# State products, folds and token-mixing subtractions on VectorE alone, in a scan, FFT and mixer kernel

## The chip, the cores and the metric

The kernel runs on one core of a Trainium2 chip. Its core has five engines that work beside one another: TensorE (PE, with weight loads on their own row, PEld), VectorE (DVE), ScalarE (ACT), GpSimd (POOL), and SyncE (SP), which issues the DMAs. The metric is the device time of one launch in microseconds (us), lower is better. Three launches of the kernel before took 1111.71, 1112.63 and 1117.65 us; the median is 1112.63 us.

## The reference

```
# q, k, v, a: 4 batches, 8 heads, 768 tokens, 48 channels (d_model = 8*48 = 384)
a_n = a * min(|a|, 0.999) / (|a| + 1e-6)          # complex decay
for t in range(768):
    S = a_n[t] * S + k[t] v[t]^T                  # complex 48x48 state per batch, head
    y[t] = q[t] @ S.real
x = y as (4, 768, 384)
mixed = real(fft over channels(fft over tokens(x)))
u = x + mixed;  un = layernorm(u)
x = u + relu(un @ w_ch1) @ w_ch2                  # 384 -> 1536 -> 384
u = x + (relu(x^T @ w_tok1) @ w_tok2)^T           # 768 -> 256 -> 768 over tokens
out = u + relu(u @ w_ch1') @ w_ch2'               # 384 -> 1536 -> 384
```

## The kernel before, in words

The four batches go one after the other through a chain, and the chain of batch b+1 runs beside the dense layers of batch b.

The chain has two stages. `stage1` first walks 49 scan steps (decay products on VectorE, L407 to L426, fed by ScalarE and GpSimd) and transposes the scaled queries and keys on TensorE (L445). Then come eight chunks of 96 tokens. For each chunk TensorE makes the scores (L511, masked on VectorE in L518), the chunk's own state (`ch_u`, L526 and L527, into PSUM) and the outputs (`ch_y`, L560 and L566, copied into `xT` by ScalarE, L568). The state is carried from chunk to chunk by five instructions in `ch_u`: `Aa` = carried state + new state (L537), three products with the complex decay of a whole chunk (`Xx` in L543, the two halves of `yc` in L544 and L545), and the sum `T` (L547), which the next chunk's L537 and L566 read.

`stage2` does the FFTs as matrix products after folding by symmetry. `xT` is folded into `xm` and `xp` (L784, difference and sum of its token halves), these into `xd` (L790), these into `fd` (L801, eight tiles of four types). TensorE multiplies the folds by cosine and sine tables (L824, L835), ScalarE and GpSimd combine the results (L871 to L873), VectorE adds them to x as `u` (L887), and the normalised rows are transposed (L708, split into a high and a low part in L711 and L712).

The dense layers are `mlp` (L728 and L744, with ScalarE's L732, VectorE's L734 and the residual sum L747), `tok1` (the input is split into `xh` on ScalarE, L933, and `xl` = u - xh, L934; then L949) and `tok2` (L967). Weights come as 64-bit patterns and are turned into two float parts per block by `convert`: ScalarE L187 and L188, VectorE L190, GpSimd L192, VectorE L195, ScalarE L201, GpSimd L202, and a DMA back to DRAM (L203). This happens once, during the chunks and folds of batch 0 and the scan of batch 1.

GpSimd's share in what the change touches: L545 for every chunk but the first, L544 also from batch 1 on; in the folds, the sum `xp` of L784, in L790 the two tiles of `xp` (batch 0) or one of them (later), in L801 two of eight tiles from batch 1 on; and L934 for every batch but 0.

Nobody writes the order of an engine's instructions out. Each instruction gets a priority from its stream (on TensorE the chain goes before dense work; on the others dense work goes first, except in batch 0) and its place in the program, and the framework fixes each engine's order ahead of time from priorities and modelled times. On the chip every engine works through its list in that order.

## Time and profile before

| What | us |
|---|---|
| median of three launches (lowest, highest) | 1112.63 (1111.71, 1117.65) |
| profiled execution, its own time | 1115.16 |
| its span, first to last instruction | 1113.4 |
| TensorE matmuls busy in the span | 991.1 (89%) |
| VectorE busy | 795.6 (71%) |
| ScalarE busy | 517.8 (47%) |
| GpSimd busy | 372.7 (33%) |
| mean granted TensorE clock, 1 = 2.4 GHz | 0.956 |

The profiled execution is 2.5 us over the median. The span starts with batch 0's chain alone (0 to 195.8 us). The first dense matmul is at 195.8; batch 1's folds start at 417.6, batch 2's at 602.2, batch 3's at 806.2; from 852 us to the end TensorE is full with dense layers that depend on no chain any more. A row of the timeline gives start, length, engine, line, operation, written tile, read tiles, shapes and the count of instructions merged into it, and in brackets how long the engine stood idle before and what ended that. A row of grouped lines gives the sum of busy time in us and the mean length in ns.

### The profile page before, as it was taken

The page shows a single profiled execution, that of the slowest core. Times are in us where ns is not written, and L with a number is a line of the kernel's source. Part 1 is how long each engine was busy: PE and PEld are TensorE (multiplying, and loading weights), DVE is VectorE, ACT ScalarE, POOL GpSimd, SP SyncE. Part 2 cuts the span into 40 slices and gives each one's busy share as a digit, 9 for nine tenths or more (in the row PEclk, how much of TensorE's full clock was granted, in tenths as well). Part 3 has the DMA queues.
Part 4 walks back from the last instruction along what each step waited for, and adds up shares of the span by engine and source line. Part 5 has one row for each costly group of instructions (what it writes and reads, how often), then busy time and mean ns, then how long its engine had stood idle before and what let it go on. Part 6 is the DMA issues. An engine that isn't in the chain of part 4 may idle for free.

```text
span 1113.4 us, 21166 instructions
## 1 busy us (share of the span) xinstructions
PE 991.1 (89%) x7322; PEld 924.0 (83%) x7322; DVE 795.6 (71%) x2161; ACT 517.8 (47%) x1442; POOL 372.7 (33%) x510
## 2 busy tenths in 40 slices
PE   1347887999889998799998999999986999999997
PEld 0126775889888897699998899999976999999997
DVE  6996897899999759899876879996565433433332
ACT  7762445777786325777522557651224212121111
POOL 4321896674567336223325312221332002000000
PEclk9997887999999999899999999999988999999999
DMA  6116973587657765264586336655421543544432
GB/s 215 41 38 137 255 265 142 177 273 235 199 190 242 213 170 190 56 202 148 175 199 184 102 99 190 191 171 149 122 79 43 158 127 115 170 142 135 163 100 74
DMA packets 102466, 174.67 MB, mean 157 GB/s; under 512 B 11216, under 2 KB 63568, under 8 KB 101840
## 3 DMA queue, kind: packets, MB, share of 16 engines
q1 hardware_dynamic: 102352, 173.24, 51.4%
q8 instruction: 60, 0.98, 0.4%
q14 instruction: 54, 0.44, 0.1%
HBM read 133.88 MB, written 39.32 MB: 156 GB/s over the span
## 4 chain that ended last, share of the span: by engine, by line
PE 64%; DVE 8%; DMA 3%; ACT 1%; POOL 1%; issue 1%; SPq 0%; POOLq 0%; DVEq 0%; ACTq 0%
PE l L744 23%; PE l L728 22%; PE s L511 3%; PE s L445 2%; DMA cvt<-wL 2%; PE s L835 2%; PE s L560 2%; PE s L824 1%; PE s L566 1%; PE s L949 1%; DVE ws L784 1%; DVE ws L790 1%; PE s L526 1%; PE s L967 1%; PE s L708 1%
## 5 line engine op out<-in xcount | busy, mean ns | idle before, releaser
L744 PE MATMUL l<-w,h 128*128 128x384 f32 x1728 | 331.0, 344 | 12.8 <-DVE h L734 8.8
L728 PE MATMUL l<-th,w 128*128 128x384 f32 x1152 | 313.8, 342 | 5.3 <-DVE h L734 2.6
L744 PEld LDWEIGHTS l<-w,h 128*128 128x128 f32 x1728 | 302.8, 191 | 17.8 <-DVE h L734 12.4
L728 PEld LDWEIGHTS l<-th,w 128*128 128x128 f32 x1152 | 210.3, 189 | 9.4 <-DVE h L734 4.4
L732 ACT ACTIVATE h<-l 128x384 fp32r<-128x384 f32 x192 | 94.1, 490 | 226.0 <-PE l L728 225.2
L728 PE MATMUL l<-tl,w 128*128 128x384 f32 x576 | 194.8, 338 | 0.0
L734 DVE SCALAR_TENSOR_TENSOR h<-l,h 128x384 fp32r<-128x384 f32 x192 | 106.1, 552 | 87.9 <-ACT h L732 87.4
L747 DVE TENSOR_TENSOR u<-u,l 128x384 f32<-128x384 f32 x192 | 105.4, 550 | 76.5 <-PE l L744 75.4
L445 PE MATMUL s<-misc,y 128*112 128x128 f32 x384 | 71.0, 306 | 60.0 <-DVE y L423 38.3
L445 PEld LDWEIGHTS s<-misc,y 128*112 128x112 f32 x384 | 50.2, 148 | 77.1 <-POOL A L384 17.6
L728 PEld LDWEIGHTS l<-tl,w 128*128 128x128 f32 x576 | 108.8, 189 | 0.7 <-DVE tl L712 0.5
L192 POOL TENSOR_TENSOR cvt<-cvt 128x384 int32<-128x384 int32 x56 | 64.4, 1156 | 37.5 <-ACT sq L351 8.1
L366 POOL TENSOR_TENSOR tm<-tm 128x144 f32<-128x144 f32 (+1 forms) x68 | 35.3, 519 | 101.1 <-ACT tm L365 100.9
L511 PE MATMUL s<-qkt 112*96 112x96 f32 x512 | 59.9, 267 | 7.4 <-DVE sc L518 6.7
L511 PEld LDWEIGHTS s<-qkt 112*96 112x96 f32 x512 | 53.6, 177 | 10.6 <-DVE sc L518 7.5
L410 DVE TENSOR_TENSOR p<-p,A 128x144 f32<-128x144 f32 x192 | 59.5, 310 | 3.0
L202 POOL TENSOR_TENSOR w<-cvt,w 128x384 fp32r<-128x384 f32 x44 | 52.6, 1204 | 8.9 <-ACT w L201 8.7
L544 POOL TENSOR_TENSOR yc<-Aa,gm 48x384 f32<-48x384 f32 x18 | 21.0, 1165 | 101.4 <-DVE Aa L537 101.4
L384 POOL TENSOR_TENSOR A<-raw,tm 128x144 f32<-128x144 f32 (+1 forms) x68 | 34.9, 513 | 59.2 <-DVE tm L382 33.2
L195 DVE SCALAR_TENSOR_TENSOR cvt<-cvt 128x384 int32<-128x384 int32 x56 | 46.8, 843 | 8.7 <-POOL cvt L192 8.5
L414 DVE TENSOR_TENSOR p<-p,yt 128x96 f32<-128x96 f32 x192 | 50.1, 261 | 3.5
L934 POOL TENSOR_TENSOR xl<-u,xh 128x384 fp32r<-128x384 f32 x18 | 18.0, 1009 | 101.1 <-ACT xh L933 101.1
(182 smaller groups left out, 1805.1 us busy)
## 6 DMA issues: line engine op xcount, KB each, us to landing
w<-wscr SPq DMA_DIRECT2D x180, 384.0 KB, 3.5
cvt<-wL SPq DMA_DIRECT2D x56, 384.0 KB, 5.1
wscr<-w SPq DMA_DIRECT2D x44, 384.0 KB, 3.7
kn<-y SPq DMA_DIRECT2D x128, 96.0 KB, 2.1
Kn<-kn SPq DMA_DIRECT2D x64, 192.0 KB, 3.9
raw<-aL SPq DMA_DIRECT2D x52, 144.0 KB, 3.1
xx<-xL SPq DMA_DIRECT2D x52, 144.0 KB, 3.1
V<-vL SPq DMA_DIRECT2D x32, 144.0 KB, 3.5
```

What stands on the lines that cost most here:

```text
L192: x = ge.tensor_tensor(out=a, in0=a, in1=lo, op=ALU.add)
L195: rest(ve.scalar_tensor_tensor(out=a, in0=hi, scalar=-0x80000000, in1=a, op0=ALU.bitwise_and, op1=ALU.bitwise_or))
L202: ge.tensor_tensor(out=parts[:, 1, :], in0=a.bitcast(F32), in1=r32(parts[:, 0, :]), op=ALU.subtract)
L410: x = ve.tensor_tensor(out=cur, in0=prev, in1=A[:, j, 0:3, :], op=ALU.mult)
L414: ve.tensor_tensor(out=cur[:, 0:2, :], in0=cur[:, 0:2, :], in1=y, op=ALU.add)
L445: te.transpose(ps[:, j, :], y[:, j, 0:112], ident)
L511: te.matmul(out=ps[:, j, :], lhsT=K[:, hc, :], rhs=Q[:, hc, :])
L728: te.matmul(out=ps, lhsT=w1[:, wi, kt * 128:kt * 128 + 128], rhs=x[g][:, kt, :], start=(n == 0), stop=(n == 8))
L732: x = se.activation(out=hi, in_=ps, func=ACTF.Relu)
L734: ve.scalar_tensor_tensor(out=h[:, 1, g * 384:g * 384 + 384], in0=ps, scalar=0.0, in1=r32(hi), op0=ALU.max, op1=ALU.subtract)
L744: te.matmul(out=ps, lhsT=hs[m][:, hi, tt * 128:tt * 128 + 128], rhs=w2[:, wi, :], start=(n == 0), stop=(n == 8))
L747: ve.tensor_tensor(out=u[tt], in0=u[tt], in1=ps, op=ALU.add)
```

## The change

Every instruction named above as GpSimd's in the chunk products, the folds and `tok1` is issued on VectorE. What is computed, all tiles and all DMAs stay the same. The three tables that held the choice go, and since one of them was a line of its own, every line number behind it is smaller by one in the changed kernel (L545 is L544 there).

```diff
-XL = (0,), (0, 1, 2, 3, 4, 5)
...
-KT, PF, PD = (0, 1), ((2, 0), (2, 1)), (((1, 0), (1, 1)), ((1, 1),))
+KT = (0, 1)
...
-            (ge if c and b else ve).tensor_tensor(out=v8(y)[0:48], in0=a[64:112], in1=gb(1, 64, 112), op=ALU.mult)
-            st["yop"] = (ge if c else ve).tensor_tensor(out=v8(y)[64:112], in0=a[0:48], in1=gb(1, 0, 48), op=ALU.mult)
+            ve.tensor_tensor(out=v8(y)[0:48], in0=a[64:112], in1=gb(1, 64, 112), op=ALU.mult)
+            st["yop"] = ve.tensor_tensor(out=v8(y)[64:112], in0=a[0:48], in1=gb(1, 0, 48), op=ALU.mult)
...
-                x1 = (ge if s else ve).tensor_tensor(out=x[:, :, o:n], in0=xT[:, :, o:n], in1=xT[:, :, 384 + o:384 + n], op=op)
+                x1 = ve.tensor_tensor(out=x[:, :, o:n], in0=xT[:, :, o:n], in1=xT[:, :, 384 + o:384 + n], op=op)
...
-                    x1 = (ge if (s, r) in PD[b > 0] else ve).tensor_tensor(out=xd[s][r][:, :, o:n], in0=x[:, 0:2, o:n], in1=x[:, 2:4, o:n], op=op2)
+                    x1 = ve.tensor_tensor(out=xd[s][r][:, :, o:n], in0=x[:, 0:2, o:n], in1=x[:, 2:4, o:n], op=op2)
...
-                    x = (ge if (ty, r) in PF and b else ve).tensor_tensor(out=fd[:, ty, r, :, lo - sh:hi - sh], in0=xd[s][r][:, :, lo:hi],
+                    x = ve.tensor_tensor(out=fd[:, ty, r, :, lo - sh:hi - sh], in0=xd[s][r][:, :, lo:hi],
...
-            (ve if b in XL[0] and i in XL[1] else ge).tensor_tensor(out=xl[i], in0=u[i], in1=r32(xh[i]), op=ALU.subtract)
+            ve.tensor_tensor(out=xl[i], in0=u[i], in1=r32(xh[i]), op=ALU.subtract)
```

With other engines and other modelled times the orders come out anew. Three places matter below.

First, VectorE in the middle of batch 0's chunks, one chunk long (`cvt` is a weight block in conversion, `sc` the masked scores). Before:

```order
L190 TENSOR_SCALAR cvt<-cvt 128x384 x2
L195 SCALAR_TENSOR_TENSOR cvt<-cvt 128x384
L537 TENSOR_TENSOR Aa<-T,l 112x384
L195 SCALAR_TENSOR_TENSOR cvt<-cvt 128x384
L543 TENSOR_TENSOR Xx<-Aa,gm_81 112x384
L544 TENSOR_TENSOR yc_80<-Aa,gm_81 48x384
L547 TENSOR_TENSOR T<-Xx,yc_80 112x384
L518 TENSOR_TENSOR sc<-s,misc 96x384 x2
```

With the change:

```order
L194 SCALAR_TENSOR_TENSOR cvt<-cvt 128x384
L189 TENSOR_SCALAR cvt<-cvt 128x384 x2
L194 SCALAR_TENSOR_TENSOR cvt<-cvt 128x384
L536 TENSOR_TENSOR Aa<-T,l 112x384
L542 TENSOR_TENSOR Xx<-Aa,gm_81 112x384
L543 TENSOR_TENSOR yc_80<-Aa,gm_81 48x384
L544 TENSOR_TENSOR yc_80<-Aa,gm_81 48x384
L546 TENSOR_TENSOR T<-Xx,yc_80 112x384
L517 TENSOR_TENSOR sc<-s,misc 96x384 x2
```

The second product now stands on VectorE between the first and the sum, which read what GpSimd made before.

Second, VectorE in batch 3's folds (`u_664x` is the dense layer's residual of batch 2). Before:

```order
L734 SCALAR_TENSOR_TENSOR h<-l,h 128x384
L784 TENSOR_TENSOR ws<-xT 112x4x288
L784 TENSOR_TENSOR ws<-xT 112x4x96
L790 TENSOR_TENSOR ws<-ws 112x2x288 x2
L747 TENSOR_TENSOR u_6643<-u_6643,l 128x384
L790 TENSOR_TENSOR ws<-ws 112x2x96 x2
L790 TENSOR_TENSOR ws<-ws 112x2x288
L747 TENSOR_TENSOR u_6644<-u_6644,l 128x384
L790 TENSOR_TENSOR ws<-ws 112x2x96
L801 TENSOR_TENSOR ws<-ws 112x2x191 x4
L747 TENSOR_TENSOR u_6645<-u_6645,l 128x384
L801 TENSOR_TENSOR ws<-ws 112x2x191 x2
```

With the change:

```order
L746 TENSOR_TENSOR u_6646<-u_6646,l 128x384
L783 TENSOR_TENSOR ws<-xT 112x4x288 x2
L783 TENSOR_TENSOR ws<-xT 112x4x96 x2
L746 TENSOR_TENSOR u_6647<-u_6647,l 128x384
L789 TENSOR_TENSOR ws<-ws 112x2x288 x2
L746 TENSOR_TENSOR u_6648<-u_6648,l 128x384
L789 TENSOR_TENSOR ws<-ws 112x2x288 x2
L789 TENSOR_TENSOR ws<-ws 112x2x96 x4
L800 TENSOR_TENSOR ws<-ws 112x2x191 x8
```

All twenty folds are VectorE's now, and of the six residual sums four stand before the folds, where before none did.

Third, TensorE at the same place, from the end of the last chunk to the first products of the folds (`l<-w,h` is a dense layer's second matmul). Before:

```order
L560 MATMUL s<-sc,V 48x96
L566 MATMUL s<-qkt,T 64x96
L566 MATMUL s<-qkt,T 48x96
L744 MATMUL l<-w,h 128x384 x45
L824 MATMUL s<-dcos,ws 128x97 x12
L744 MATMUL l<-w,h 128x384 x9
L824 MATMUL s<-dcos,ws 128x97 x4
```

With the change:

```order
L559 MATMUL s<-sc,V 48x96
L565 MATMUL s<-qkt,T 64x96
L565 MATMUL s<-qkt,T 48x96
L743 MATMUL l<-w,h 128x384 x14
L823 MATMUL s<-dcos,ws 128x97 x16
L823 MATMUL s<-dcos,ws 64x97 x8
L823 MATMUL s<-dcos,ws 65x97 x4
```

Of the 54 dense matmuls that stood behind the last chunk 14 are left there; the other 40 now come earlier. Counted the same way over the whole list, the dense matmuls issued by the end of the last chunk are 876 before and 879 now in batch 1, 1473 and 1506 in batch 2, 2250 and 2290 in batch 3.

## Rows read from the trace of the kernel before

**Rows 1.** Windows: start:end, length, then PE, PEld, DVE, ACT, POOL busy, clock, DMA.

```profile
0.00:195.80 195.80, 118.73 (x963) 91.25 (x963) 161.82 (x452) 109.23 (x315) 103.69 (x143) 0.87 0.53 155
417.60:463.70 46.10, 35.41 (x205) 29.55 (x206) 41.33 (x122) 27.92 (x87) 23.03 (x32) 0.87 0.42 131
463.70:602.20 138.50, 138.45 (x1261) 133.84 (x1260) 111.51 (x346) 73.51 (x214) 39.51 (x67) 0.99 0.60 168
602.20:806.20 204.00, 200.74 (x1626) 191.64 (x1627) 162.18 (x484) 103.14 (x303) 56.89 (x92) 0.98 0.53 153
806.20:852.10 45.90, 34.05 (x196) 28.85 (x197) 30.52 (x65) 16.67 (x45) 19.19 (x18) 0.84 0.15 49
```

**Rows 2.** The same view for batch 0's later chunks and folds.

```profile
107.50:161.90 54.40, 46.10 (x553) 40.39 (x552) 50.64 (x76) 24.36 (x55) 47.41 (x38) 0.82 0.94 286
```

**Rows 3.** Grouped lines of VectorE in that stretch.

```profile
L544 DVE TENSOR_TENSOR yc<-Aa,gm 48x384 f32<-48x384 f32 x6 | 7.4, 1240 | 0.1
L547 DVE TENSOR_TENSOR T<-Xx,yc 112x384 f32<-112x384 f32 x6 | 6.5, 1078 | 1.3 <-POOL yc L545 0.7
...
L801 DVE TENSOR_TENSOR ws<-xd 112x382 f32<-112x382 f32 x8 | 6.2, 842 | 0.0
...
L543 DVE TENSOR_TENSOR Xx<-Aa,gm 112x384 f32<-112x384 f32 x6 | 5.9, 980 | 0.0
L790 DVE TENSOR_TENSOR xd<-xf 112x192 f32<-112x192 f32 x8 | 5.0, 674 | 0.0
```

**Rows 4.** Grouped lines of GpSimd in that stretch.

```profile
L202 POOL TENSOR_TENSOR w<-cvt,w 128x384 fp32r<-128x384 f32 x8 | 13.8, 1735 | 0.0
L192 POOL TENSOR_TENSOR cvt<-cvt 128x384 int32<-128x384 int32 x10 | 12.4, 1252 | 0.4
L790 POOL TENSOR_TENSOR xd<-xf 112x192 f32<-112x192 f32 x8 | 6.8, 876 | 0.1
L545 POOL TENSOR_TENSOR yc<-Aa,gm 48x384 f32<-48x384 f32 x6 | 6.6, 1100 | 33.8 <-DVE Aa L537 31.3 <-ACT w L201 2.3
L784 POOL TENSOR_TENSOR xf<-xT 112x384 f32<-112x384 f32 x4 | 5.8, 1462 | 0.0
```

**Rows 5.** Timeline: VectorE's products and folds where GpSimd was idle.

```profile
105.04 0.55 DVE L545 TENSOR_TENSOR yc<-l,gm 48x384 f32<-48x384 f32 x1
...
427.37 0.75 DVE L790 TENSOR_TENSOR ws<-ws 112x576 f32<-112x576 f32 x1
...
816.76 0.35 DVE L790 TENSOR_TENSOR ws<-ws 112x192 f32<-112x192 f32 x1
```

**Rows 6.** Grouped lines of VectorE in batch 3's folds, 806.2 to 822.2 us.

```profile
L784 DVE TENSOR_TENSOR ws<-xT 112x384 f32<-112x384 f32 x1 | 3.0, 3034 | 0.0
...
L784 DVE TENSOR_TENSOR ws<-xT 112x1152 f32<-112x1152 f32 x1 | 1.4, 1357 | 1.7 <-PE s L566 1.7
```

**Rows 7.** Timeline of TensorE in the folds of batches 1, 2 and 3.

```profile
418.59 3.29 PE L744 MATMUL l<-w,h 128*128 128x384 f32 x18
424.90 4.75 PE L744 MATMUL l<-w,h 128*128 128x384 f32 x18 [3.02 <-DVE h L734]
...
438.12 2.53 PE L824 MATMUL s<-dcos,ws 112*64 112x97 f32 x24 [0.92 <-ACT ws L826]
...
608.01 2.33 PE L744 MATMUL l<-w,h 128*128 128x384 f32 x8 [2.07 <-DVE h L734]
611.54 3.57 PE L744 MATMUL l<-w,h 128*128 128x384 f32 x10 [1.19 <-DVE h L734]
...
814.42 6.10 PE L744 MATMUL l<-w,h 128*128 128x384 f32 x18 [3.42 <-DVE u L747]
...
824.62 4.13 PE L824 MATMUL s<-dcos,ws 112*128 112x97 f32 x40
```

**Rows 8.** Timeline of GpSimd: the first combination in batch 0, and tok1's subtractions.

```profile
179.26 0.53 POOL L872 TENSOR_TENSOR ws<-ws 128x193 f32<-128x193 f32 x1
...
843.24 5.77 POOL L934 TENSOR_TENSOR xl<-u,xh 128x384 fp32r<-128x384 f32 x6 [2.84 <-ACT xh L933]
```

## The prediction

> **What bounds the kernel now.** I read the windows first, cut where the chains meet the dense layers. In the first 195.8 us TensorE is busy for 118.7 and part of that is filler: batch 0's chain runs alone and VectorE, busy for 161.8, sets the pace [rows 1]. Between the folds of batches 1 and 2 and again up to those of batch 3 the picture turns round: TensorE is busy for 138.45 of 138.50 us, then for 200.74 of 204.00, so there only its amount of work counts. The windows of batch 1's and batch 3's folds are the other kind: 35.41 of 46.10 us and 34.05 of 45.90 busy, a clock of 0.87 and 0.84, TensorE waiting for the chain [rows 1]. So the change is paid or earned in four places, batch 0's chunks and folds and three later folds, and TensorE's order decides what is carried between them.
>
> Next the grouped lines of batch 0's stretch. VectorE is busy for 50.64 of 54.40 us and GpSimd for 47.41 [rows 2]: both are full, which looks as if nothing could move. But the lengths say otherwise. A product of 384 columns takes 0.55 us where GpSimd is idle [rows 5]; in this stretch L544 takes 1.24, L547 1.08 and L543 0.98, L801 0.84, and L790's 192 columns 0.67 instead of 0.35 [rows 3, 5]. In batch 3's folds the 384-column L784 takes 3.03 us while the one with 1152 columns before it takes 1.36 [rows 6]. What these share is that both inputs lie in SBUF and that GpSimd runs beside them.
>
> That is a lock and not a slow operation, and the Trainium skill says so (SBUF — State Buffer, "Who interferes with whom"): a VectorE instruction with two SBUF inputs and a GpSimd instruction that reads SBUF hold one port pair in turns, each for its whole length. The trace agrees with the 3.03 against 0.55 us.
>
> **The change, step by step.** It is priced against the profiled execution, 1115.2 us.
>
> *A, batch 0's chunks and folds.* GpSimd loses six L545, four L784 and eight L790: 6.6 + 5.8 + 6.8 = 19.2 us of its 47.4 [rows 2, 4]. VectorE gains ten instructions at 0.55 and eight at 0.35, 8.3 us [rows 5]. How much of VectorE's waiting goes is what the trace does not show, so I bound it. Its waits in these rows are 6 x 0.69 + 6 x 0.53 + 6 x 0.43 + 8 x 0.29 + 8 x 0.32 = 14.8 us, and 54.4 - 50.6 = 3.8 us of idleness come on top: 18.6. GpSimd keeps its twenty conversions there. If waits fall only as its work falls, by 19.2 of 47.4 or 40%, VectorE saves 7.5 and the change costs 0.8. If the two were strictly in turns, all 19.2 go for 8.3: a gain of 10.9. I take a gain of 4.5, near the middle: behind the chunks GpSimd has no conversion left in its list until the folds are through, so the folds run at VectorE's own prices, while in the chunks the conversions still take their turns. The conversions behind the folds, which keep GpSimd until L872 at 179.26 [rows 8], are as many as before and only shift. **-4.5.**
>
> *B, from there to batch 1's folds.* No changed instruction but batch 1's chunk products; three more dense matmuls stand ahead of the folds, at 3.29 / 18 = 0.18 us [rows 7]. **+0.5.**
>
> *C, batch 1's folds.* TensorE's dense work stops for 3.02 us for an L734 that stands behind L784 and L790, and restarts slowly: 18 matmuls in 4.75 us against 3.29 [rows 7]. With the change that L734 comes behind four L784 and one L790 and ends 2 x 1.36 + 2 x 0.55 + 0.75 + 0.55 = 5.1 us after the folds begin, where TensorE now goes on after 424.90 - 417.60 = 7.3, and all folds cost VectorE 3.8 + 4 x 0.75 + 4 x 0.35 + 8 x 0.55 = 12.6 us without a wait [rows 5, 6]. TensorE's last L824 now ends at 440.65, 23.0 us after the start [rows 7]. After the change the 57 dense matmuls left ahead of it (of 936 by then) need 57 x 0.18 = 10.3 us and a wait of about 1, and 64 products at 4.13 / 40 = 0.10 us bring that to some 18: about 4.5 us sooner at best. ScalarE's copies already cost 0.92 us there, so I take 3.5, with 1.5 as the poor end. **-3.5.**
>
> *D, up to batch 2's folds.* TensorE is full, and 1506 instead of 1473 dense matmuls stand ahead of the folds; batch 1 started level, so 33 x 0.18 = **+5.9.** The two products of each chunk and batch 1's six L934 come to VectorE here, but it is busy for only 111.5 of 138.5 us [rows 1], and TensorE's full list hides them; without that cover the 18 chunks of three batches would cost 18 x 2 x 0.55 = 20 us and each batch's L934 3.3.
>
> *E, batch 2's folds and up to batch 3's.* Between the two folds 784 dense matmuls replace 777, +1.3. TensorE stops there now for 2.07 and 1.19 us for L734, and the 18 matmuls behind these take 5.90 us instead of 3.1 [rows 7]: 6.1 us lost. With the change the residual sums stand between the folds instead, and TensorE has three accumulators to run ahead with; I expect about 1.6 us of standstill and 1 of slow restart. So -3.5 + 1.3 = **-2.2**, between -4.8 (nothing lost) and +1.3 (as much as now).
>
> *F, batch 3's folds to the end of its chain.* Only 14 dense matmuls are left here, so TensorE is through them after 2.4 us and idles until the first folds are made, at 3.8 + 4.4 + 2 x 0.55 + 1.1 = 10.4 us. Its restart runs at the lower clock level: after 3.42 us of idleness now, 18 matmuls took 6.10 us, 0.34 each, which is 1.2 instead of 2.4 GHz [rows 7]. The last fold is due at 12.6 + 1.1 = 13.7 us, forty L824 follow at 0.10, plus 1 to 3 us for the slow part: near 19.5 us, where it is 828.75 - 806.2 = 22.5 now. The six L934 among the norm's small steps cost VectorE 6 x 0.55 = 3.3 us in place of a GpSimd run of 5.77 us [rows 8] that held them up; I set that even. **-3.0**, between -6 and +3.
>
> Behind 852 us all is TensorE's and unchanged; SP's list only swaps neighbours. The sum is -4.5 + 0.5 - 3.5 + 5.9 - 2.2 - 3.0 = **-6.8 us**: 1108.4 for the profiled execution, and since the median of 1112.6 lies 2.5 below that one, 1105.8 for the median. A measurement of this kernel tells about 0.5% from no change, 5.6 us, so 1107.0 and 1118.2 are the bounds.
>
> **The rivals.**
>
> *Slower: the filler is spent too early.* TensorE's dense work is what fills the folds. The new order puts 40 of its matmuls ahead of batch 3's folds, where TensorE is full, and takes them from a stretch where it would otherwise stand. Then D's 5.9 and E's 1.3 are paid in full, E's 6.1 comes back at the new standstill, F's idleness of some 8 us makes all 64 L824 run at 0.2 us, 10.4 + 12.8 + 2 of copies = 25.2 against 22.5 and so about +3, and C keeps 1.5: -4.5 + 0.5 - 1.5 + 5.9 + 1.3 + 3 = +4.7, so 1117.3. For it: the counts, the full windows and the slow restarts [rows 1, 7]. Against it: the folds get shorter whatever TensorE does. It decides once TensorE's gap before batch 3's first L824 passes the 3.42 us of now by more than the folds' gain.
>
> *The same: VectorE is saturated in batch 0.* A is +0.8, with the conversions taking every freed turn; with the others as forecast -1.5, so 1111.1. For it: VectorE's 50.64 of 54.40 and GpSimd's 26 us of conversions [rows 2, 4]. The Trainium skill (Perfetto Trace Analysis, "Optimizing Scalar/DVE Operations") speaks for it too: work may be offloaded to GpSimd where VectorE is saturated, though the shared port may spoil that. The 0.55 against 1.24 us says here that it does.
>
> *Much faster: strict turns.* A at -10.9, C at -4.5, E at -4.8, F at -6: with B and D -19.8, so 1092.8. By the rule of the SBUF page, taken to the letter for every instruction, A is this -10.9 and the sum with the rest as forecast -13.2, an estimate. Against it: VectorE's 50.6 us less its 14.8 of waits and GpSimd's 47.4 make 83 in a stretch of 54.4 [rows 2, 3], so much of GpSimd's time was not VectorE's loss.
>
> **How the numbers follow.** Forecast 0.45, slower rival 0.20, same rival 0.20, much faster 0.15. The forecast is good to about 5 us, so 0.28 of it is faster by over 0.5% and 0.17 within; the same rival gives 0.05, 0.13 and 0.02; the slower one 0.02, 0.04 and 0.14; the last is all faster. Faster 0.50, same 0.34, slower 0.16. The range leaves out half of the fast case and a little of the slow one: 1095 to 1119.
>
> **What would show it.** In the new profile L543, L544 and L547 of batch 0's chunks should still show waits, about 0.8 us each, and L790 and L801 0.35 and 0.55; the first dense matmul should come at 191 instead of 195.8. Batch 1's first to last fold should take about 14 us and its last L824 end within 20. Batch 2's folds should begin some 1 to 2 us earlier than 602.2 and show no idle row over 2 us; batch 3's should begin near 802 and show a long gap of TensorE before the first L824. I am wrong if the first dense matmul does not come earlier, if the fold windows are no shorter, or if TensorE shows gaps between 464 us and batch 3's folds that it does not have now.

## The result, and the profile after

The changed kernel is slower: 1125.78 us (median of four launches, 1125.23 to 1129.05) against 1112.17 us (four launches of before), a ratio of 1.0115 with a 95% interval of 1.0090 to 1.0141. The prediction was 1105.8 us, with 1095 to 1119 as its range. The profiled execution of the changed kernel took 1125.23 us, its span is 1123.4 us against 1113.4: 10.0 us more, which is what the views below can account for. The other 3.6 us of the medians' difference lie in the choice of the profiled executions: that of before is 3.0 us above its median, that of the changed kernel 0.6 below.

The first part of the page gives busy time, share and instructions of each engine: GpSimd lost 102 us of work, VectorE gained 24, TensorE is as before.

```profile
PE 988.2 (88%) x7322; PEld 922.6 (82%) x7322; DVE 819.7 (73%) x2251; ACT 514.5 (46%) x1442; POOL 271.0 (24%) x420
```

The windows of the changed kernel, cut at its own landmarks (columns as in [rows 1]):

```profile
0.00:202.80 202.80, 115.64 (x963) 89.99 (x963) 165.19 (x471) 110.01 (x315) 83.63 (x125) 0.88 0.51 150
107.50:161.90 54.40, 42.40 (x548) 38.24 (x547) 52.91 (x95) 24.98 (x55) 26.68 (x20) 0.86 0.94 284
174.90:187.70 12.80, 12.23 (x34) 7.74 (x33) 4.26 (x9) 2.33 (x6) 7.65 (x9) 0.50 0.73 274
425.10:467.50 42.40, 33.49 (x200) 27.22 (x200) 37.80 (x124) 26.20 (x83) 13.09 (x23) 0.88 0.44 143
467.50:617.20 149.70, 147.05 (x1295) 142.42 (x1296) 124.69 (x373) 74.93 (x221) 22.75 (x51) 0.98 0.57 161
617.20:818.80 201.60, 199.70 (x1633) 190.41 (x1633) 165.86 (x502) 101.29 (x300) 37.31 (x74) 1.00 0.52 151
818.80:863.40 44.60, 30.10 (x157) 24.52 (x157) 25.96 (x74) 16.67 (x45) 3.05 (x6) 0.74 0.14 51
```

Held against [rows 1], the prediction's six stretches and the rest behind batch 3's chain come out so:

| Stretch | before | changed | difference | forecast |
|---|---|---|---|---|
| A: to the first dense matmul | 195.8 | 202.8 | +7.0 | -4.5 |
| B: to batch 1's folds | 221.8 | 222.3 | +0.5 | +0.5 |
| C: to the next dense matmul | 46.1 | 42.4 | -3.7 | -3.5 |
| D: to batch 2's folds | 138.5 | 149.7 | +11.2 | +5.9 |
| E: to batch 3's folds | 204.0 | 201.6 | -2.4 | -2.2 |
| F: to the end of batch 3's chain | 45.9 | 44.6 | -1.3 | -3.0 |
| the rest | 261.3 | 260.0 | -1.3 | 0 |

B, C and E are as forecast. In TensorE's timeline C's pauses are 1.64 and 0.37 us where one of 3.02 stood [rows 7], and F has the long pause before the first fold product that was expected:

```profile
430.47 3.39 PE L743 MATMUL l<-w,h 128*128 128x384 f32 x18 [1.64 <-DVE h L733]
434.23 3.42 PE L743 MATMUL l<-w,h 128*128 128x384 f32 x18 [0.37 <-DVE u L746]
437.49 7.12 PE L823 MATMUL s<-dcos,ws 112*128 112x97 f32 x64
...
828.77 12.21 PE L823 MATMUL s<-dcos,ws 112*128 112x97 f32 x64 [7.44 <-ACT ws L807]
```

The loss is in A and D.

**A, up to the last fold.** The window from 107.5 to 161.9 us ends with the last fold in both kernels: nothing was won. The last sum of the chunks (L546) ends at 150.1 us instead of 149.0 (L547), and what the chunks lost the folds won back. Single executions differ here: in seven profiles whose order is that of before up to the last fold it ends at 160.2 to 161.9 us (mean 161.1), in five with the changed order at 159.2 to 162.1 (mean 160.9). GpSimd's work in the window fell from 47.4 to 26.7 us, VectorE's rose from 50.6 to 52.9 [rows 2]. VectorE's grouped lines there say why, and behind them stands all that GpSimd still does:

```profile
L543 DVE TENSOR_TENSOR yc<-Aa,gm 48x384 f32<-48x384 f32 x6 | 7.6, 1271 | 0.1
L544 DVE TENSOR_TENSOR yc<-Aa,gm 48x384 f32<-48x384 f32 x6 | 6.9, 1155 | 0.1
L546 DVE TENSOR_TENSOR T<-Xx,yc 112x384 f32<-112x384 f32 x6 | 6.1, 1015 | 0.2
...
L542 DVE TENSOR_TENSOR Xx<-Aa,gm 112x384 f32<-112x384 f32 x6 | 5.0, 838 | 0.1
L789 DVE TENSOR_TENSOR xd<-xf 112x192 f32<-112x192 f32 x16 | 4.6, 349 | 0.0
...
L800 DVE TENSOR_TENSOR ws<-xd 112x382 f32<-112x382 f32 x8 | 3.8, 555 | 0.0
```

```profile
L191 POOL TENSOR_TENSOR cvt<-cvt 128x384 int32<-128x384 int32 x10 | 12.8, 1294 | 29.4 <-DMA Kn<-kn 29.4
L201 POOL TENSOR_TENSOR w<-cvt,w 128x384 fp32r<-128x384 f32 x8 | 10.3, 1286 | 11.3 <-ACT w L200 8.5 <-DMA Kn<-kn 2.7
L201 POOL TENSOR_TENSOR cvt<-cvt 128x384 fp32r<-128x384 f32 x2 | 3.9, 1964 | 3.0 <-ACT cvt L200 3.0
```

The folds came down to VectorE's own prices, 0.35 and 0.55 us [rows 3, 5]. The products of the chunks did not: L543, the L544 of before, takes 1.27 us where it took 1.24, and the moved product L544 takes 1.16. GpSimd's conversions, twenty instructions as before, took the turns that its products had left.

**A, behind the last fold.** From there to the first dense matmul it took 34.0 us before and takes 41.0. This difference is steady: in the four other runs below whose batch 0 is that of before it takes 33.6 to 33.8 us, in two with the changed batch 0 40.9 and 42.1. TensorE's timeline (start, length):

```profile
169.52 0.83 PE L823 MATMUL s<-dcos,ws 112*65 112x97 f32 x8
173.90 1.09 PE L823 MATMUL s<-dcos,ws 112*63 112x97 f32 x8 [3.54 <-ACT ws L825]
174.92 3.83 PE L834 MATMUL s<-ws 128*128 128x193 f32 x8
...
180.25 6.86 PE L834 MATMUL s<-ws 128*128 128x193 f32 x16
...
201.34 1.51 PE L707 MATMUL s<-misc,ws 128*128 128x128 f32 x6 [4.36 <-DVE ws L915]
```

The last tile of the fold products waits 3.54 us for L825, the copy that frees a PSUM buffer, and the work behind that pause runs at half the clock: the window 174.9 to 187.7 has a granted clock of 0.50. ScalarE's timeline shows where the copy was:

```profile
168.41 0.32 ACT L825 COPY ws<-s 128x194 f32<-128x194 f32 x1
169.47 0.51 ACT L200 CAST cvt<-cvt 128x384 fp32r<-128x384 f32 x1 [0.74 <-DVE cvt L194]
170.76 0.51 ACT L200 CAST cvt<-cvt 128x384 fp32r<-128x384 f32 x1 [0.78 <-DVE cvt L194]
173.11 0.51 ACT L200 CAST cvt<-cvt 128x384 fp32r<-128x384 f32 x1 [1.83 <-DVE cvt L194]
173.53 0.54 ACT L825 COPY ws<-s 64x194 f32<-64x194 f32 x2
```

It stands behind three casts of conversions, which wait for VectorE's L194. Beside GpSimd's conversions L194 takes 1.22 us on average (155 to 203 us); in the chunks it took 0.54. The change names no instruction of ScalarE; the order of its list came out anew.

**D.** Of the 11.2 us, 34 more matmuls (1295 against 1261, 33 of them dense) make some 6. TensorE stops once, for 2.7 us, and the granted clock is lower in two places: 0.53 for 3.6 us behind the stop, which costs 1.7 us, and 0.51 in the first 4.0 us of the stretch, where it was 0.79 before, another 1.1. These four make 11.4. The stop is a wait for batch 2's keys. First the waits of TensorE in this stretch, then VectorE's timeline, then the queue of SP:

```profile
PE s L525 <- issue: 2.7, 1, 2.7
```

```profile
547.45 0.55 DVE L933 TENSOR_TENSOR xl<-u,xh 128x384 fp32r<-128x384 f32 x1
...
556.26 0.56 DVE L933 TENSOR_TENSOR xl<-u,xh 128x384 fp32r<-128x384 f32 x1 [0.46 <-ACT xh L932]
...
558.97 0.45 DVE L425 TENSOR_TENSOR y<-xx,p 128x288 f32<-128x288 f32 x1
```

```profile
561.19 0.45 SPq L427 DMA_DIRECT2D kn<-y  x1
561.81 1.13 SPq L501 DMA_DIRECT2D Kn<-kn  x2
...
568.03 0.82 SPq L501 DMA_DIRECT2D Kn<-kn  x2
```

The six subtractions of `tok1` (L933) now stand among the last scan steps, the last of which (L425) starts 91.5 us after the stretch does, where before it was 86.8. Its keys go out at 561.19, are read back from 568.03 on, and TensorE has them at 572.6, 105.2 us after the start of the stretch; before, it went on without a wait at 96.3. So only 4.7 of these 8.9 us are the scan's. The rest is the way through DRAM: the write of the last keys (KB, then us from issue to landing), before and now, is

```profile
kn<-y SPq DMA_DIRECT2D x1, 96.0 KB, 3.2
```

```profile
kn<-y SPq DMA_DIRECT2D x1, 96.0 KB, 6.8
```

No run shows why that write took longer.

### The profile page after: what moved, and what is told of

Same layout as the page of the kernel before. It is cut to its first block, busy times and chain, and to the rows that moved or that the text cites. A ratio compares the mean times of both kernels' runs of the same rounds, so it can differ in the third digit from the quotient of the medians.

```text
span 1123.4 us, 21091 instructions
## 1 busy us (share of the span) xinstructions
PE 988.2 (88%) x7322; PEld 922.6 (82%) x7322; DVE 819.7 (73%) x2251; ACT 514.5 (46%) x1442; POOL 271.0 (24%) x420
## 4 chain that ended last, share of the span: by engine, by line
PE 63%; DVE 12%; ACT 3%; issue 2%; DMA 2%; POOL 1%; SPq 0%; POOLq 0%; DVEq 0%; ACTq 0%
PE l L727 22%; PE l L743 22%; PE s L510 3%; PE s L823 2%; PE s L444 2%; PE s L559 2%; DVE cvt L194 1%; PE s L834 1%; PE s L565 1%; PE s L948 1%; PE s L966 1%; PE s L525 1%; DVE ws L783 1%; DVE u L746 1%; DVE ws L789 1%
## 5 line engine op out<-in xcount | busy, mean ns | idle before, releaser
L743 PE MATMUL l<-w,h 128*128 128x384 f32 x1728 | 324.9, 339 | 6.0 <-DVE h L733 4.0
L727 PE MATMUL l<-th,w 128*128 128x384 f32 x1152 | 317.6, 344 | 6.3 <-DVE u L746 3.2
L743 PEld LDWEIGHTS l<-w,h 128*128 128x128 f32 x1728 | 297.6, 188 | 11.0 <-DVE h L733 6.4
L355 POOL TENSOR_TENSOR tm<-sq 128x144 f32<-128x144 f32 (+1 forms) x68 | 38.6, 569 | 137.8 <-ACT sq L350 132.3
L201 POOL TENSOR_TENSOR w<-cvt,w 128x384 fp32r<-128x384 f32 x44 | 49.5, 1133 | 30.9 <-ACT w L200 27.9
L412 DVE TENSOR_TENSOR yt<-p,A 128x96 f32<-128x96 f32 x192 | 48.4, 252 | 2.6
L194 DVE SCALAR_TENSOR_TENSOR cvt<-cvt 128x384 int32<-128x384 int32 x56 | 47.4, 853 | 2.2 <-POOL cvt L191 2.2
```

Of the source, the lines that this page charges most:

```text
L194: rest(ve.scalar_tensor_tensor(out=a, in0=hi, scalar=-0x80000000, in1=a, op0=ALU.bitwise_and, op1=ALU.bitwise_or))
L201: ge.tensor_tensor(out=parts[:, 1, :], in0=a.bitcast(F32), in1=r32(parts[:, 0, :]), op=ALU.subtract)
L727: te.matmul(out=ps, lhsT=w1[:, wi, kt * 128:kt * 128 + 128], rhs=x[g][:, kt, :], start=(n == 0), stop=(n == 8))
L743: te.matmul(out=ps, lhsT=hs[m][:, hi, tt * 128:tt * 128 + 128], rhs=w2[:, wi, :], start=(n == 0), stop=(n == 8))
```

## The experiments

Each ratio is against runs of the kernel before on the same chip, whose medians were 1113.5 to 1115.1 us. The table has the stretches' lengths, as in the table above, from each run's profiled execution, with the ratio and its interval. One execution is not the median: later_folds and l934_alone have the orders of before up to batch 1's folds and reach them 4.7 and 4.3 us earlier, with A shorter by 1.7 and 1.6 us. So differences of 1 to 2 us in A and of 3 in B show nothing.

| Run | A | B | C | D | E | F | ratio |
|---|---|---|---|---|---|---|---|
| before | 195.8 | 221.8 | 46.1 | 138.5 | 204.0 | 45.9 | |
| changed | 202.8 | 222.3 | 42.4 | 149.7 | 201.6 | 44.6 | 1.0115 (1.0090 to 1.0141) |
| b0_alone | 202.4 | 221.4 | 46.4 | 143.2 | 204.1 | 47.4 | 1.0131 (1.0095 to 1.0166) |
| products_batch0 | 197.5 | 220.5 | 46.1 | 138.8 | 203.8 | 45.8 | 1.0045 (1.0026 to 1.0064) |
| folds_batch0 | 196.8 | 223.2 | 45.9 | 143.6 | 202.6 | 47.6 | 1.0059 (1.0035 to 1.0082) |
| later_alone | 194.4 | 221.2 | 44.9 | 147.5 | 201.4 | 44.6 | 1.0027 (1.0012 to 1.0042) |
| products_later | 195.6 | 222.1 | 46.8 | 143.4 | 207.5 | 48.6 | 1.0116 (1.0091 to 1.0142) |
| later_folds | 194.1 | 218.9 | 44.2 | 141.7 | 200.3 | 45.9 | 0.9980 (0.9959 to 1.0001) |
| l934_alone | 194.2 | 219.2 | 46.1 | 142.1 | 205.1 | 46.9 | 1.0051 (1.0026 to 1.0076) |
| without_l934 | 204.2 | 221.7 | 42.4 | 144.3 | 201.1 | 45.8 | 1.0062 (1.0038 to 1.0086) |
| copies_first | 192.8 | 222.0 | 51.5 | 146.8 | 201.4 | 43.9 | 1.0093 (1.0058 to 1.0129) |
| fill_the_pause | 200.1 | 219.1 | 46.1 | 144.9 | 201.0 | 44.8 | 1.0058 (1.0041 to 1.0075) |
| later_folds_all_sums | 196.7 | 222.5 | 49.5 | 146.5 | 199.5 | 41.0 | 1.0083 (1.0066 to 1.0100) |
| folds_and_copies | 194.4 | 219.7 | 47.1 | 140.9 | 201.2 | 41.4 | 0.9955 (0.9935 to 0.9976) |

**b0_alone: batch 0's part of the change.** Against before:

```diff
-            st["yop"] = (ge if c else ve).tensor_tensor(out=v8(y)[64:112], in0=a[0:48], in1=gb(1, 0, 48), op=ALU.mult)
+            st["yop"] = (ge if c and b else ve).tensor_tensor(out=v8(y)[64:112], in0=a[0:48], in1=gb(1, 0, 48), op=ALU.mult)
...
-                x1 = (ge if s else ve).tensor_tensor(out=x[:, :, o:n], in0=xT[:, :, o:n], in1=xT[:, :, 384 + o:384 + n], op=op)
+                x1 = (ge if s and b else ve).tensor_tensor(out=x[:, :, o:n], in0=xT[:, :, o:n], in1=xT[:, :, 384 + o:384 + n], op=op)
...
-                    x1 = (ge if (s, r) in PD[b > 0] else ve).tensor_tensor(out=xd[s][r][:, :, o:n], in0=x[:, 0:2, o:n], in1=x[:, 2:4, o:n], op=op2)
+                    x1 = (ge if (s, r) in PD[b > 0] and b else ve).tensor_tensor(out=xd[s][r][:, :, o:n], in0=x[:, 0:2, o:n], in1=x[:, 2:4, o:n], op=op2)
```

> Only batch 0's chunk products and folds go to VectorE; later batches and L934 are as before. Theory (the loss lies in batch 0's order): the engines' orders from 103 to 195 us are those of the changed kernel, so the first dense matmul comes at 202 to 203 us instead of 195.8, with TensorE's pause of about 3.5 us before the last products of the folds and a clock near 0.5 behind it; 20 more dense matmuls stand ahead of batch 2's folds, 20 x 0.18 = 3.6 us; together 1119 to 1123 us. Rival (the loss lies in the later batches, where VectorE carries more): first dense matmul by 197 us and the whole within 1110 to 1115 us.

1129.11 us, above the theory's 1123, with the first dense matmul at 202.4 us and 4.7 us more in D (21 dense matmuls more, and no stop). Batch 0's part alone costs as much as the whole change.

**products_batch0 and folds_batch0: its two halves,** the first pair of lines of that diff, and the other two.

> Only batch 0's chunk products (L544 here, the second half) go to VectorE; all counts of dense matmuls are those of before. Theory (on VectorE the added product waits for GpSimd's conversions like the others, and nothing is won): the last fold ends at 161 to 164 us as before (161.8), the first dense matmul comes at 196 to 200 us, the whole takes 1112 to 1118 us. Rival (VectorE wins the turns that GpSimd gives up, as the prediction had it): last fold 2 us earlier, first dense matmul at 194 us or before, 1111 us or less.

> Only batch 0's folds go to VectorE. On ScalarE the casts (L200) then stand between the copies of the fold products (L825) at six places. Theory (the folds themselves get shorter, the copies behind the casts take that back and more): last fold at 160 to 162 us, TensorE pauses of 1 us or more among L823, first dense matmul at 196 to 203 us, 1115 to 1122 us in all. Rival (the folds alone are what the prediction hoped for, the loss comes from the chunk products): first dense matmul at 193 us or before, 1112 us or less.

1120.64 and 1122.76 us, both above the expected range. With the products alone the last fold ends at 161.9 us (161.8 before): nothing won. With the folds alone it ends at 159.5, in this one execution 1.6 us below the mean of the seven with the old order and 0.7 below the earliest of them. From the last fold to the first dense matmul the two take 35.6 and 37.2 us instead of 34.0. So the folds win a little, and the stretch behind takes it back, though not as expected: with the folds alone TensorE pauses among L823 for only 1.02 us. It loses the time further on, waiting 6.68 us for the third pair of normalised rows (L915), which on VectorE now comes behind a new conversion. The profiled execution of products_batch0 took 1115.83 us, 4.8 below its median, so its row does not show where its 5.0 us go.

**later_alone, products_later, later_folds, l934_alone: the later batches' part, whole and in pieces.** Against before, in this order the products, the folds and L934; later_alone has all three:

```diff
-            (ge if c and b else ve).tensor_tensor(out=v8(y)[0:48], in0=a[64:112], in1=gb(1, 64, 112), op=ALU.mult)
-            st["yop"] = (ge if c else ve).tensor_tensor(out=v8(y)[64:112], in0=a[0:48], in1=gb(1, 0, 48), op=ALU.mult)
+            ve.tensor_tensor(out=v8(y)[0:48], in0=a[64:112], in1=gb(1, 64, 112), op=ALU.mult)
+            st["yop"] = (ge if c and not b else ve).tensor_tensor(out=v8(y)[64:112], in0=a[0:48], in1=gb(1, 0, 48), op=ALU.mult)
...
-                x1 = (ge if s else ve).tensor_tensor(out=x[:, :, o:n], in0=xT[:, :, o:n], in1=xT[:, :, 384 + o:384 + n], op=op)
+                x1 = (ge if s and not b else ve).tensor_tensor(out=x[:, :, o:n], in0=xT[:, :, o:n], in1=xT[:, :, 384 + o:384 + n], op=op)
...
-            (ve if b in XL[0] and i in XL[1] else ge).tensor_tensor(out=xl[i], in0=u[i], in1=r32(xh[i]), op=ALU.subtract)
+            ve.tensor_tensor(out=xl[i], in0=u[i], in1=r32(xh[i]), op=ALU.subtract)
```

(L790 gets `and not b` in the same way, and L801 is `ve`.)

> Batch 0 as before; the chunk products and folds of batches 1 to 3 and L934 go to VectorE. Theory: the first dense matmul stays at 195.8 us; batch 1's folds win about 3.7 us, batch 3's about 1.3; from there to batch 2's folds it takes about 150 us instead of 138.5, with a stop of TensorE of about 2.7 us before batch 2's first state product L525, because L933 stands among the last scan steps on VectorE; 1113 to 1117 us in all. Rival (the loss lies in the later batches): 1122 us or more.

> Only the chunk products of batches 1 to 3 go to VectorE. Theory (their time is hidden by TensorE's full list, but the order that comes out puts 21 dense matmuls more ahead of batch 2's folds and 18 more between these and batch 3's): first dense matmul at 194 to 196 us, 142 us to batch 2's folds instead of 138.5, 206 to 207 us to batch 3's instead of 204, 1116 to 1120 us. Rival (hidden, and the order costs nothing, since a dense matmul that comes earlier is missing later): within 2 us of before in all, 1112 to 1116 us.

> Only the folds of batches 1 to 3 go to VectorE, the rest is as before. Theory (the folds' gain is real, and small beside what the other parts cost): the first dense matmul stays at 194 to 196 us, batch 1's folds take about 42.5 to 45 us to the next dense matmul instead of 46.1, the way to batch 2's folds 142 us with 21 more dense matmuls ahead (21 x 0.18 = 3.8) and no stop before L525, the last two segments win 2 to 3 us: 1109 to 1114 us, level with before or up to 4 below. Rival (VectorE is full there too, so folds on it come late): segment of batch 1's folds no shorter than 46 us, 1117 us or more.

> Only L934 (L933 here) of batches 1 to 3 goes to VectorE. Theory (it stands among the last scan steps and makes batch 2's keys late): 22 more dense matmuls ahead of batch 2's folds (4.0 us), a stop of TensorE of 1 to 3 us before batch 2's first L525, 145 to 149 us from the end of batch 1's folds to batch 2's folds instead of 138.5; 1118 to 1123 us. Rival (six instructions of 0.55 us per batch are hidden where TensorE is full): that stretch at most 142 us and the whole within 4 us of before.

later_alone took 1117.52 us, just above the expected 1117: D 9.0 us longer with a stop of 1.5 us before L525, C and E shorter. So the loss is not mainly in the later batches, where they stand alone.

products_later took 1127.72 us, more than expected. E is 3.5 us longer, as the eighteen dense matmuls at 0.18 said, D 4.9 and F 2.7. TensorE's timeline in F:

```profile
815.18 2.53 PE L743 MATMUL l<-w,h 128*128 128x384 f32 x13
827.85 12.61 PE L823 MATMUL s<-dcos,ws 112*128 112x97 f32 x64 [10.14 <-ACT ws L807]
```

Thirteen dense matmuls are left, TensorE stands for 10.14 us, and its 64 fold products take 0.20 us each instead of 0.10 [rows 7]. This is the rival "the filler is spent too early", in full.

later_folds took 1111.23 us, level with before or a little faster: C 1.9 and E 3.7 us shorter, D 3.2 longer. l934_alone took 1118.12 us. D is 142.1 us, 22 matmuls at 0.16, and there is no stop to speak of (0.12 us before L525, the last scan step 89.2 us into the stretch): there my theory of the late keys fell, and the rival's 142 held but for 0.1, while the whole still lost more than the rival's 4 us.

**without_l934: the change but for `tok1`.** Against the changed kernel:

```diff
-            ve.tensor_tensor(out=xl[i], in0=u[i], in1=r32(xh[i]), op=ALU.subtract)
+            (ge if b else ve).tensor_tensor(out=xl[i], in0=u[i], in1=r32(xh[i]), op=ALU.subtract)
```

> The whole change but for tok1's subtraction (L933 here), which stays on GpSimd for batches 1 to 3. Theory: batch 0 as in the changed kernel (first dense matmul at 202 to 203 us); no stop of TensorE before batch 2's L525, and 142 to 144 us from batch 1's end to batch 2's folds instead of 149.7; 1117 to 1121 us in all, some 6 below the changed kernel. Rival (33 dense matmuls ahead of their time cost the 11 us, whatever VectorE does): the stretch stays at 147 us or more, and the whole above 1123.

1122.54 us, between the two sides' ranges. D is 144.3 us without a stop, 5.4 less than in the changed kernel; the scan's last step comes 2.4 us earlier in the stretch. But the order changed too: 23 instead of 33 more dense matmuls stand ahead of batch 2's folds, 1.8 us at 0.18. So L934's subtractions make up about half of D's 11.2, a third of that by the order; they stop TensorE only together with the products and folds (later_alone), and which of these it takes no run shows.

**no_conversions: who holds the products?**

```diff
-CF = (2, 2, 2, 2, 2, 0, 8, 0)
+CF = (0, 0, 0, 0, 0, 0, 0, 0)
```

> The changed kernel with no weight block converted during batch 0's chunks and folds: all are converted behind them. Theory (VectorE's products wait for GpSimd's conversions, which take the turns that the moved products left): L542, L543, L544 and L546 take 0.55 us each in batch 0's chunks instead of 1.2 to 1.3, a chunk's period falls from 7 us to 4 to 5. Rival (the products are slow for another reason, their broadcast operand or TensorE's PSUM traffic): they stay at 1 us or more. The whole is longer, since the conversions come later.

VectorE's grouped lines from 104 to 124 us, five chunks:

```profile
L546 DVE TENSOR_TENSOR T<-Xx,yc 112x384 f32<-112x384 f32 x5 | 2.8, 558 | 0.2
L542 DVE TENSOR_TENSOR Xx<-Aa,gm 112x384 f32<-112x384 f32 x5 | 2.8, 557 | 0.2
...
L543 DVE TENSOR_TENSOR yc<-Aa,gm 48x384 f32<-48x384 f32 x5 | 2.8, 553 | 0.1
L544 DVE TENSOR_TENSOR yc<-Aa,gm 48x384 f32<-48x384 f32 x5 | 2.8, 551 | 0.1
```

All at 0.55 us, a chunk every 4.0 us instead of 7.7, the last fold at 140.1 us and the first dense matmul at 172.9. The conversions are what holds the products. They have to be paid elsewhere: from the first dense matmul to batch 2's folds it takes 448.2 us, 41.7 more than before, and the one launch took 1129.59 us.

**copies_first and fill_the_pause: the end of batch 0.** The first orders the casts of the conversions behind the copy of the last sum on ScalarE; the second only gives TensorE something to do in the pause:

```diff
-        se.copy(out=parts[:, 0, :], in_=a.bitcast(F32))
+        rest2(se.copy(out=parts[:, 0, :], in_=a.bitcast(F32)))
...
-            for _ in range(5):
-                tick(0)
-            rests[0] = None
...
-                se.copy(out=cc, in_=ps)
+                zz = se.copy(out=cc, in_=ps)
...
+                if b == 0 and i == 2:
+                    rests[2] = zz
+                    for _ in range(5):
+                        tick(0)
+                    rests[0] = rests[2] = None
```

```diff
-                n0, n = 128 * kt, ZK[ty][kt]
+                n0, n = 128 * kt, ZK[ty][kt]; b == 0 and (kt, ty) == (1, 3) and warm(30, ident)
```

(`rest2(x)` puts x behind `rests[2]` in the order, with no wait on the chip; `warm` issues L304.)

> The changed kernel, but behind batch 0's folds the conversions' ScalarE cast (L200) is ordered after the copies of the fold products (L825) and of the three sums (L870). Theory (TensorE waits for copies that stand behind casts, and then runs at the lower clock): no pause over 1 us of TensorE before its last L823, L834's eight matmuls take about 2.2 us instead of 3.8, the first dense matmul comes at 188 to 193 us instead of 202.8, and the whole takes 1112 to 1117 us. Rival (VectorE's eighteen added instructions and the lock make batch 0 longer, the copies' place does not matter): first dense matmul at 200 us or later, 1123 us or more.

> The changed kernel with thirty dummy transposing matmuls (L304) put before the last of the eight tiles of batch 0's fold products, where TensorE paused for 3.54 us; nothing else is edited, the copies stay behind the casts. Theory (the pause costs twice: itself, and the lower clock behind it): without idleness of over 1 us there, L834's first eight matmuls take 2.2 us instead of 3.83 and the next sixteen 3.8 instead of 6.86, the clock from 175 to 188 us is over 0.9 instead of 0.50, and the first dense matmul comes at 196 to 199 us instead of 202.8. Rival (the clock falls there whatever TensorE does before): L834 as slow as in the changed kernel, first dense matmul at 202 us or later.

copies_first, TensorE's timeline:

```profile
168.40 2.16 PE L834 MATMUL s<-ws 128*128 128x193 f32 x8
...
171.54 3.77 PE L834 MATMUL s<-ws 128*128 128x193 f32 x16
...
426.28 1.13 PE L823 MATMUL s<-dcos,ws 112*128 112x97 f32 x8 [0.79 <-ACT ws L807]
431.10 11.28 PE L823 MATMUL s<-dcos,ws 112*128 112x97 f32 x56 [3.68 <-ACT ws L807]
```

The order of copies and casts decides A: no pause, L834 at full clock, the first dense matmul at 192.8 us, 10.0 earlier than in the changed kernel. Of that 2.7 us were there at the last fold, ahead of the edit; from the last fold on it takes 33.6 us instead of 41.0, as long as in the kernel before. The edit does more than free the copies, though: GpSimd's halves of the conversions (L201) hang on the casts and come later too, so its first combination (L871) starts at 171.21 instead of 180.60 us. How much either does isn't separated. The whole, 1123.25 us, is not below 1117, since C is 9.1 us longer than in the changed kernel: with 49 instead of 57 dense matmuls left behind the last chunk's output TensorE ran dry among batch 1's folds, and 56 products ran at 0.20 us each.

fill_the_pause (1120.60 us):

```profile
171.93 0.88 PE L823 MATMUL s<-dcos,ws 112*63 112x97 f32 x8 [0.42 <-ACT ws L825]
172.74 2.16 PE L834 MATMUL s<-ws 128*128 128x193 f32 x8
...
198.50 1.51 PE L707 MATMUL s<-misc,ws 128*128 128x128 f32 x6 [6.21 <-DVE ws L915]
```

The copies come as late as they did, the pause is filled, and the granted clock from 174.9 to 187.7 us is 1.00 instead of 0.50. TensorE's first L707 comes at 187.43 instead of 193.71 us, 6.3 earlier, 2.0 of which were there at the last fold. So the pause and its clock cost 4.3 us up to there. The first dense matmul comes 2.7 earlier, 0.7 without those 2.0, where 4 to 7 were expected: the third pair of normalised rows (L915) waits on VectorE behind new conversions, as in folds_batch0.

**folds_and_copies, later_folds_all_sums, folds_sums_first: which mixture is best?** All have copies_first's edit on the kernel before, in the first run with `i == 0` in its condition, in the second 2, in the third 1; the first two add later_folds' edit, the third puts all folds of all batches on VectorE.

> The folds of batches 1 to 3 on VectorE as in the run of these alone, and behind batch 0's folds the conversions' casts (L200) ordered after the copies of the fold products and of the first sum on ScalarE; all else as before. Theory (the order of copies and casts sets batch 0's end, and the folds win in later batches): first dense matmul at 191 to 195 us, batch 1's folds 42 to 45 us, 11 more dense matmuls ahead of batch 2's folds than before (about 140.5 us), 1104 to 1110 us. Rival (what batch 0 wins is lost in batch 1's folds, where the dense work has run out): batch 1's folds 48 us or more with TensorE waiting among its L823, 1112 us or more.

> The folds of batches 1 to 3 on VectorE, batch 0's folds as before, and the conversions' casts ordered after all copies of batch 0's fold products and sums. Only 43 dense matmuls are left for batch 1's folds instead of 60. Theory (the work that fills batch 1's folds is spent, TensorE pauses and its L823 run at half the clock, as in the run with the copies first): first dense matmul at 187 to 191 us, batch 1's folds 49 to 52 us, 1106 to 1112 us. Rival (the folds on VectorE alone are short enough): batch 1's folds at most 46 us, 1100 to 1105 us.

> All folds of all batches on VectorE, chunk products and L934 as before, and the conversions' casts ordered after the copies of the fold products and of the first two sums. Theory (GpSimd's subtractions of the conversions, L201, no longer stand before the second sum, and batch 1's folds keep 61 dense matmuls for themselves): first dense matmul at 188 to 193 us, batch 1's folds 42 to 47 us, batch 2's folds reached in 140 to 142 us, 1102 to 1108 us. Rival (won in batch 0, lost again in batch 1's folds): batch 1's folds 49 us or more, 1109 us or more.

folds_and_copies took 1108.47 us and beats both kernels, by 0.45% (0.24 to 0.65) against before. Its gain is not where I put it: the first dense matmul comes at 194.4 us, where others with the old order stand, C is 47.1, and none of the eleven dense matmuls moved ahead of batch 2's folds, but E and F are 2.8 and 4.5 us shorter. In F 53 dense matmuls are left as before, TensorE does not pause before batch 3's fold products, and these take 7.12 us. later_folds_all_sums took 1123.34 us: C 49.5 as the theory had it, but D 146.5 with a stop of 2.3 us for the keys, which neither side had, and without any L934 on VectorE. folds_sums_first took 1113.44 us, a ratio of 0.9988 (0.9966 to 1.0009), so the theory's time is missed and the rival's holds; its profiled execution took 1124.34 us, 10.9 above the median, and is not read.

## Why the prediction was wrong

**Step A failed, in both its halves.** For the chunks and folds it put the gain at -4.5, between +0.8 ("waits fall only as its work falls") and -10.9 ("strictly in turns"). Measured up to the last fold: 0.0 (0.2 won by the means of seven and five executions), near the poor end. I had the lock right and the turns wrong: 20 conversions of GpSimd are there before and after, and no_conversions shows that without them VectorE's products run at their own price. The far end was too far besides: it took 19.2 us of waiting away where its rows have 18.6. That "in the chunks the conversions still take their turns" stood in the text; it should have set the price. Only the folds, which run while GpSimd has no conversion, came down to their own prices, and the chunks, about 1 us longer, took that back.

The larger half is the sentence that the conversions behind the folds "are as many as before and only shift", at a cost of nothing. They did not only shift: ScalarE's order changed, copies came behind casts, TensorE paused for 3.54 us and lost its clock: +7.0 us. copies_first shows the place of the conversions' casts to be the cause: with them behind the copies the stretch takes 33.6 us again. fill_the_pause shows that the pause and the clock are 4.3 us of it up to the first L707; but filling them brings the first dense matmul only 0.7 us, since VectorE's normalisation then waits behind new conversions. How A's 7.0 us divide between TensorE's clock, GpSimd's turns and VectorE's list stays open. The prediction read VectorE's and TensorE's new orders and left ScalarE's unread, at the place where it expected its largest gain.

**Step D was mis-sized,** 11.2 instead of 5.9. The counted part held: 5.9 us for the dense matmuls. Missing were 2.7 us of stop and 2.8 of lower clock, behind the stop and at the start of the stretch. The prediction said of L934 that "TensorE's full list hides them"; the list hides instructions, but not that the scan on which the next batch's keys hang ends 4.7 us later. That alone would not have stopped TensorE, which had 29 more dense matmuls ahead of L525, 5.2 us; 4.2 us on the keys' way through DRAM came on top. without_l934 removes the stop and half of D. A stop before the first L525 stands in the four profiles with products, folds and L934 all on VectorE (0.3 to 2.7 us) and in later_folds_all_sums (2.3), whose last scan step is not late at all; no run changed the keys' way by itself, so this cause is argued and not shown.

**Steps C and E held,** mechanism and all: batch 1's last L823 ends 19.5 us after its folds begin ("within 20"), and among batch 2's folds TensorE stands for 1.9 us in all where 1.6 were expected. **F** won 1.3 instead of 3.0: TensorE stood for 7.44 us, as expected, but all 64 L823 then ran at half the clock (12.21 us), where the forecast let forty run at 0.10 us each; that price was in the slower rival. Where 53 dense matmuls are left instead of 13 and the folds are on VectorE, as in folds_and_copies, F takes 41.4 us. That B held to 0.1 is luck, since it differs by 3 us between executions of equal orders.

**The rivals.** "VectorE is saturated in batch 0" described the chunks rightly. "The filler is spent too early" gave the right sign at a chance of 0.20. Its mechanism is at work in the whole change, in D's 5.9 us and in F, which is 3.2 us longer than in folds_and_copies; but C, E and F still came out shorter than before, and the largest losses, A and the other half of D, are not its. products_later shows it in full. Neither rival, nor I, had the pause behind the folds.

**The parts do not add up.** By their ratios the five single parts cost 5.0, 6.6, 12.9, -2.2 and 5.7 us, 28 together, the whole 12.8. Batch 0's two halves nearly do (11.6, and 14.6 for both in b0_alone); the later three do not (16.4, and 3.0 for all in later_alone). Four of the five lose 3 to 5 us in D, and all but the products of batch 0 put 21 to 23 more dense matmuls ahead of batch 2's folds, where the whole change puts 33. So in D they pay for one thing, once. And products_later's 2.7 us in F are gone in later_alone, where the folds on VectorE are ready sooner.

## What to carry to other kernels

Work taken off an engine buys time on its neighbour only if nothing else in that engine's list takes the turns; count what is left in the list there, not what was removed. Where a scheduler sorts anew, read the order of every engine behind the point of the change, above all of the one that frees buffers: here the copies that came to stand behind casts, with what hangs on these, cost 7 us, more than all of batch 0's folds won. And work that fills a later standstill is worth what the standstill costs, its clock included; here some twenty matmuls that moved ahead cost about 4 us, and in three of the four single parts that moved them nothing came back.

## What was not expected of the hardware

TensorE ran at half speed behind its pauses among the fold products: after 2.64 us (64 L823 in 13.33 us, in later_folds_all_sums), 3.54 (granted clock 0.50), 3.68 (56 L823 in 11.28), 7.44 (64 in 12.21) and 10.14 (64 in 12.61). With the one of 3.54 filled, and 0.42 us of idleness left, the clock stayed at 1.00 from 174.9 to 187.7 us. Before batch 3's fold products eleven profiles have a pause, of 4.49 to 10.14 us, and there the 64 L823 take 11.5 to 12.6 us; in four without a pause they take 7.1 to 8.4. Not every fall has a long pause before it: in the kernel before, behind 0.73 and 1.02 us of idleness, the clock from 182.2 to 195.8 us is 0.50 too.

A small VectorE instruction can wait for a whole GpSimd instruction: in fill_the_pause the same L906 on 128x2 numbers takes 0.16 us alone and 0.92 beside an L201 of 0.99 that started 0.09 us before it.

```profile
183.44 0.16 DVE L906 SCALAR_TENSOR_TENSOR rs<-mv,rs 128x2 f32<-128x2 f32 x1
...
196.09 0.92 DVE L906 SCALAR_TENSOR_TENSOR rs<-mv,rs 128x2 f32<-128x2 f32 x1
```

The Trainium skill (SBUF — State Buffer, "SBUF: two separate sides") says that the lock is held for the whole instruction; the trace agrees. The step of 0.16 us waits for 0.76 us, as long as a product of 0.55 us that takes 1.27.
